# Float16 high and low parts for both layers of a spectral block, in place of float32r

## The chip, the cores and the metric

The kernel runs on one core of one Trainium2 chip. The metric is the device time of one execution in microseconds. The engines of the core have in-order instruction streams of their own: TensorE (PE in the profile, its weight loads PEld), VectorE (DVE), ScalarE (ACT), GpSimd (POOL), and SyncE (SP), which issues the DMA transfers.

## The reference, cut to what matters

x has 8192 rows of 448 columns. With `mod` computed from `c` and `w_mod`, the spectral part is

```python
h = _layernorm(x, axis=-1) * (1 + ca) + sa
Xf = rfft2(h)                            # over the 8192 rows and (length 1) H
z = Xf.reshape(..., NB=4, BS=112)        # 4 blocks of 112 columns
hr = zr @ w1[0] - zi @ w1[1] + b1[0];  hi = zi @ w1[0] + zr @ w1[1] + b1[1]
hr, hi = relu(hr), relu(hi)
or_ = hr @ w2[0] - hi @ w2[1] + b2[0]; oi_ = hi @ w2[0] + hr @ w2[1] + b2[1]
or_, oi_ = soft thresholds with lam = 0.01: sign(o) * max(|o| - lam, 0)
x = x + ga * irfft2(or_ + 1j * oi_)
```

Then a second layer norm with modulation and a GEGLU feed-forward of width 1792 follow, which the change does not touch.

## The kernel before, in words

The Fourier transform of 8192 rows is split into 128 x 64. The first stage (to about 72 us of the profile) normalizes the rows, multiplies by `f1` (the transform of length 128) and stores the result `td` to DRAM. The spectral stage, to about 376 us, works in 32 units: two halves h of the columns (two blocks of 112 each) by 16 groups `bt` of frequencies, in the order of `BTS`. Each unit passes through four functions:

- `stage_s2`: the transform of length 64, 24 float16 matmuls. For each of two blocks kk, ScalarE writes `zhi` (float32r, scaled by `ca1`, a scalar of each partition), VectorE the rest `zlo` = value - `zhi`.
- `stage_m1`: the first layer. Each real or imaginary output is six float32r matmuls of 256 columns, with high and low parts of weights (`w1h`, `w1l`) and data; 24 in a unit. ScalarE writes relu to `hhi`, VectorE `hlo`.
- `stage_m2`, for two halves p of the unit's frequencies: the second layer, six matmuls of 224 columns for each block, 24 in a unit. ScalarE makes `t` = relu(value - lam), VectorE in four instructions `y` = min(value + lam, t); together they are the soft threshold.
- `stage_i1`: the inverse transform of length 64, six float32r matmuls of 448 columns; ScalarE copies the result to `us`.

The order of instructions is written by hand (`manual_schedule`). `step(i)` issues the fetch of unit i + 2, `stage_s2` of unit i, `stage_m2` of unit i - 2, `stage_i1` of unit i - 3 and `stage_m1` of unit i - 1. The table `side` hangs work of the next part on the steps: `squares` (ScalarE, one in each of steps 4 to 15, two in steps 12 and 13, with `norms` matmuls a step later) and `weights_hi` and `weights_lo` (ScalarE and VectorE, one each in steps 18 to 31, names `wk<-raw`). I call these squares steps and weights steps; steps 16 and 17 have neither. `drip` issues small leftovers.

In a step ScalarE's order is zh, zh (of `stage_s2`), th (the float16 copy of the next fetched unit), squares or `weights_hi`, t, t (of `stage_m2`), yh, us, us, yh, hh, hh (of `stage_m1`). VectorE's is zl, zl, y eight times, the step's side work (`weights_lo` in a weights step), hl, hl.

Before the first step stands the preparation: `mod_cols` sums the modulation into columns (TensorE, then `sa0` and `ca1` on VectorE), `mod_rows` makes rows `sb_r` and `cb_r` for the second layer norm, `mlp_weights` splits the weights on VectorE, constant rows are written into the four `zh` and the four `hh` buffers, and `split_t` makes th and tl of units 0 and 1 from the fetched `tr`, tl on VectorE for these two. The bank of PSUM that `stage_s2` of unit 0 fills is free for unit 1 once ScalarE and VectorE have made zh and zl from it.

Of the kernel before, what the change touches and what calls it, by code (L numbers as in the profile page):

```python
# [45 lines left out]
SSC = 14  # L46


@with_exitstack
def spectral_geglu(ctx, tc, x, w1, b1, w2, b2, wg, wu, wd, cvec, wmod, cf1, cs2, cmi, cgm, out):  # L50
# [23 lines left out]
    nlam = cpool.tile([128, 1], F32, name="nlam")  # L74
    V.memset(nlam, -LAM)
# [67 lines left out]
    with ExitStack() as actx:  # L143
# [91 lines left out]
        def mod_rows():  # L235

            out = []
            for h, r in enumerate((sb_r, cb_r)):
                ps = bank("pd", "psm")
                for k in range(4):  # L240
                    T.matmul(
                        ps[:, :D], cs[:, k : k + 1].to_broadcast([112, 128]), wn[:, k, h * D : (h + 1) * D], start=k == 0, stop=k == 3
                    )
# [1710 lines left out]
```

## Time and profile before

| | |
|---|---|
| median of three runs | 1883.52 us (1882.44 to 1884.96) |
| profiled execution, its own span | 1881.0 us |
| TensorE matmul busy | 1841.5 us, 98% |
| VectorE, ScalarE, GpSimd busy | 74%, 53%, 68% |
| mean granted TensorE clock | 0.996 |
| first stage, spectral stage, the rest | to 72, 72 to 376, 376 to 1881 us |

Matmuls are pipelined and the profile models their ends, so TensorE looks busy whenever starts are less than some 0.25 us apart. For its real pace one reads the distance of starts in the timeline. A row of the timeline has start, length, engine, line, operation, tiles and in brackets the idle time before it with what ended it; several instructions of a line in a row are merged with a count.

### The profile page before, as it was taken

How to read it: one execution, taken by the hardware profiler on the slowest of the kernel's cores; microseconds unless marked ns; L12 is line 12 of the kernel's file. 1: busy time of each engine (PE TensorE's matmuls, PEld its weight loads, DVE VectorE, ACT ScalarE, POOL GpSimd, SP SyncE). 2: the span in 40 equal slices, each digit the busy share in tenths (PEclk: the TensorE clock that was granted, in tenths of full speed). 3: DMA queues.
4: the chain of work that ended last, by engine and by line, in shares of the span. 5: the costliest groups of instructions: out<-in, count | busy, mean ns of one | idle time of the engine just before them, and what ended most of it. 6: DMA issues, size and time to landing. Idle time of an engine off the chain costs nothing.

```text
span 1881.0 us, 56421 instructions
## 1 busy us (share of the span) xinstructions
PE 1841.5 (98%) x23332; PEld 1748.9 (93%) x23332; DVE 1397.2 (74%) x2887; ACT 1000.7 (53%) x1844; POOL 1271.3 (68%) x1684
## 2 busy tenths in 40 slices
PE   7899999999999999999999999999999999999998
PEld 3599999878889989999999999999999999999998
DVE  7777788787766667777777777777777777777745
ACT  5677888753444444455555555555555555444443
POOL 3157654347777778777777777777777777777534
PEclk9999999999999999999999999999999999999999
DMA  9999777754543445966666666666666666666651
GB/s 350 319 301 262 204 183 189 192 157 92 133 107 88 101 96 125 291 177 178 175 172 169 169 169 169 169 169 169 173 177 178 170 173 180 176 173 179 155 162 55
DMA packets 380614, 330.49 MB, mean 176 GB/s; under 512 B 110784, under 2 KB 358724, under 8 KB 380356
## 3 DMA queue, kind: packets, MB, share of 16 engines
q1 hardware_dynamic: 380356, 326.87, 63.9%
q8 instruction: 183, 3.00, 0.7%
q14 instruction: 75, 0.61, 0.1%
HBM read 243.32 MB, written 60.10 MB: 161 GB/s over the span
## 4 chain that ended last, share of the span: by engine, by line
PE 82%; DVE 6%; DMA 3%; issue 3%; ACT 2%; SPq 2%; POOL 2%; ACTq 0%; DVEq 0%; POOLq 0%
PE set L1391 39%; PE pgu L1148 11%; PE pdn L1221 6%; PE pdn L1223 6%; PE pdn L1222 6%; PE ps L211 2%; PE set L1223 2%; PE set L1222 2%; PE set L1221 2%; DVE y L479 1%; POOL yl L116 1%; DVE st L172 1%; PE set L1515 1%; DMA raw<-in_B_w_gate 1%; DVE wk L838 1%
## 5 line engine op out<-in xcount | busy, mean ns | idle before, releaser
L1391 PE MATMUL set<-nt,wk 128*128 128x128 f16 x13104 | 736.5, 219 | 2.8 <-DMA wk<-wk 1.6
L1391 PEld LDWEIGHTS <-wk 128*128 128x128 f16 x13104 | 733.9, 98 | 3.2 <-DMA wk<-wk 1.8
L1223 PE MATMUL pdn<-wd,ac 128*128 128x224 f16 x1218 | 315.5, 259 | 0.6 <-DVE ac L1209 0.6
L1221 PE MATMUL pdn<-wd,ac 128*128 128x224 f16 x1218 | 315.7, 259 | 0.0
L1222 PE MATMUL pdn<-wd,ac 128*128 128x224 f16 x1218 | 315.5, 259 | 0.0
L1148 PE MATMUL pgu<-nt,wk 128*128 128x256 f16 (+1 forms) x2464 | 268.3, 274 | 3.1 <-DVE x L1189 3.1
L1148 PEld LDWEIGHTS <-wk 128*128 128x128 f16 (+1 forms) x2464 | 225.8, 98 | 44.2 <-issue 18.3
L1440 ACT ACTIVATE gl<-c,dg 128x384 f32<-128x384 f32 x168 | 103.5, 616 | 230.6 <-DVE c L1434 227.7
L1466 DVE SCALAR_TENSOR_TENSOR ac<-x,sa_act,ac 128x896 f16<-128x896 f32 x168 | 205.8, 1225 | 19.9 <-ACT ac L1456 19.9
L1197 POOL TENSOR_TENSOR x<-x 128x128 f32<-128x128 f32 x223 | 129.8, 582 | 117.6 <-DVE x L1189 56.2
L1267 POOL TENSOR_TENSOR cq<-cq 128x224 f32<-128x224 f32 x32 | 21.1, 659 | 261.8 <-DVE cq L1266 261.8
L1198 POOL TENSOR_TENSOR x<-x 128x128 f32<-128x128 f32 x223 | 185.6, 832 | 17.5
L1456 ACT ACTIVATE ac<-x,sa_act 128x896 f16<-128x896 f32 x168 | 174.1, 1036 | 13.5 <-POOL x L1200 6.6
L1444 DVE TENSOR_TENSOR x<-c,gl 128x384 f32<-128x384 f32 x168 | 154.4, 919 | 17.2 <-ACT gl L1440 17.1
L1221 PEld LDWEIGHTS <-ac 128*128 128x128 f16 x1568 | 153.4, 98 | 4.9 <-issue 4.8
L1223 PEld LDWEIGHTS <-ac 128*128 128x128 f16 x1568 | 153.4, 98 | 0.8 <-DVE ac L1209 0.8
L1222 PEld LDWEIGHTS <-ac 128*128 128x128 f16 x1568 | 153.5, 98 | 0.1
L1428 DVE TENSOR_TENSOR c<-set,sb 128x512 f32<-128x512 f32 x168 | 115.4, 687 | 35.7 <-PE set L1391 35.7
L1199 POOL TENSOR_TENSOR x<-x 128x128 f32<-128x128 f32 x223 | 134.0, 601 | 0.0
L1184 ACT ACTIVATE gel<-pgu,dg 128x256 f32<-128x256 f32 x112 | 49.4, 470 | 156.7 <-PE pgu L1148 149.1
L1419 ACT COPY sb<-set 128x512 f32<-128x512 f32 x168 | 97.6, 581 | 61.8 <-PE set L1391 60.4
L479 DVE SCALAR_TENSOR_TENSOR y<-pm,t 64x224 f32<-64x224 f32 x256 | 99.5, 389 | 39.1 <-ACT t L471 35.2
(338 smaller groups left out, 3998.8 us busy)
## 6 DMA issues: line engine op xcount, KB each, us to landing
wk<-wk SPq DMA_DIRECT2D x76, 1024.0 KB
wk<-wk SPq DMA_DIRECT2D x76, 768.0 KB
vd<-us SPq DMA_DIRECT2D x64, 224.0 KB
xx<-in_A_x SPq DMA_DIRECT2D x32, 448.0 KB
v<-vd SPq DMA_DIRECT2D x63, 224.0 KB
out<-x SPq DMA_DIRECT2D x31, 448.0 KB
xt<-in_A_x SPq DMA_DIRECT2D x15, 896.0 KB
tr<-td SPq DMA_DIRECT2D x60, 224.0 KB
```

Source lines behind the costliest of these rows:

```text
L479: V.scalar_tensor_tensor(y[ri * 64 : ri * 64 + 64, gi], pv[si, ri], LAM, tv[si, ri], op0=ALU.add, op1=ALU.min)
L1148: T.matmul(pgu[i, t, q][:, pr * H : (pr + 1) * H], ws[rows, n, w, tw], nts[i][rows, tn, :], start=start, stop=stop, skip_group_check=True,)
L1197: e.tensor_tensor(s1, a21, a22, ALU.add)
L1198: e.tensor_tensor(s2, s1, a11, ALU.subtract)
L1199: e.tensor_tensor(s3, a11, a21, ALU.subtract)
L1221: T.matmul(ps, ac[:, 0, ka], w[:, 0, kb], start=n == 0, stop=False)
L1222: T.matmul(ps, ac[:, 0, ka], w[:, 1, kb], start=False, stop=False)
L1223: T.matmul(ps, ac[:, 1, ka], w[:, 0, kb], start=False, stop=n == NP - 1)
L1391: T.matmul(ps2[:, pr, reg * 128 : reg * 128 + 128], slot[:, pr, hl, wt, :], nt[:, xt, :], start=start and j == 0, stop=j == len(terms) - 1 ...
L1444: V.tensor_tensor(xs[u][:, 1::3, :], cts.pop(u)[:, 1], gls.pop(u), ALU.mult)
L1456: S.activation(ac[:, 0], xs[u][:, 0:7], AF.Copy, scale=sa_act[:, t : t + 1])
L1466: V.scalar_tensor_tensor(ac[:, 1], xs.pop(u)[:, 0:7], sa_act[:, t : t + 1], ac[:, 0], op0=ALU.mult, op1=ALU.subtract)
```

## The change

The data and weights of both layers (`zh`, `zl`, `hh`, `hl`, `w1h`, `w1l`, `w2h`, `w2l`) become float16. Since float16 has a narrow range, powers of two scale them. The factor 1 + ca now goes into the first weights (`w1m`), so `zh` and `zl` get a constant scale; the shift sa comes in as an addition `hb` to the hidden value at frequency 0. The scales `wsc` of the two layers are made on the chip: a bound of each layer's weights (`wmx`, `cmx`, `cm`) is squared, summed over the partitions by a matmul with ones (`psq`), and turned into a power of two by integer operations on its exponent. The thresholds change with the scales, so `lam` becomes a tile, and `ga_r` takes the inverse scale `iso`.

```diff
-    w1h = mpool.tile([113, 3, NBLK, BS], F32R, name="w1h")
+    w1h = mpool.tile([113, 3, NBLK, BS], F16, name="w1h")
...
+        def dc_cols():
+
+            ps = bank("pc", "psd")
+            for r in range(2):
+                for k in range(NBLK):
+                    T.matmul(ps[:112, 4 * r + k : 4 * r + k + 1], wt[:112, 0, r, k, :], sa0[:, k : k + 1], start=True, stop=True)
+            return lambda: V.tensor_scalar(hb, ps[:112, : 2 * NBLK], wsc[:112, 0:1], None, op0=ALU.mult)
+
+        def bounds1():
+
+            V.tensor_reduce(cmx[:112, 0:1], ca1[:112], mybir.AxisListType.X, ALU.max, apply_absolute_value=True)
+            V.tensor_reduce(cmx[:112, 1:2], sa0, mybir.AxisListType.X, ALU.max, apply_absolute_value=True)
+            V.scalar_tensor_tensor(
+                cm[:112, 0:1], cmx[:112, 1:2], 2.0**ZSC / N, cmx[:112, 0:1], op0=ALU.mult, op1=ALU.add
+            )
+            V.tensor_tensor(cm[:, 0:1], cm[:, 0:1], wmx[:, 0:1], ALU.mult)
+            V.tensor_tensor(cm[:, 0:1], cm[:, 0:1], cm[:, 0:1], ALU.mult)
+            V.tensor_tensor(
+                w1m, wt[:, 0], ca1.rearrange("p (r k o) -> p r k o", r=1, o=1).to_broadcast([113, 2, NBLK, BS]), ALU.mult
+            )
+
+        def scale_of(j, p):
+
+            ps = bank("pc", "psq")
+            T.matmul(ps[:, 0:1], ones[:113, :128], cm[:, j : j + 1], start=True, stop=True)
+            w = wsc[:, j : j + 1]
+            wi = w.bitcast(I32)
+            V.tensor_scalar(w, ps[:, 0:1], 1e-20, None, op0=ALU.max)
+            V.tensor_scalar(wi, wi, 1, 0x7F800000, op0=ALU.logical_shift_right, op1=ALU.bitwise_and)
+            V.tensor_scalar(wi, wi, -1.0, float((189 + p) << 23), op0=ALU.mult, op1=ALU.add)
+
+        def weights1():
+            sc = wsc[:113, 0:1]
+            S.activation(w1h[:, 0:2], w1m, AF.Copy, scale=sc)
+            V.scalar_tensor_tensor(w1l[:, 0:2], w1m, sc, w1h[:, 0:2], op0=ALU.mult, op1=ALU.subtract)
+            for w in (w1h, w1l):
+                neg(w[:112, 2], w[:112, 1])
+
+        def bounds2():
+
+            V.scalar_tensor_tensor(col2, f1c[:113, 129:130], wsc[:113, 0:1], f1c[:113, 128:129], op0=ALU.mult, op1=ALU.add)
+            V.tensor_tensor(cm[:, 1:2], wmx[:, 1:2], col2, ALU.mult)
+            V.tensor_tensor(cm[:, 1:2], cm[:, 1:2], cm[:, 1:2], ALU.mult)
+
+        def weights2():
+            V.tensor_tensor(col2, col2, wsc[:113, 1:2], ALU.mult)
+            wr = wt[:, 1].rearrange("p r k o -> p k r o")
+            wv = [w.rearrange("p s k (r o) -> p s k r o", r=2) for w in (w2h, w2l)]
+            S.activation(wv[0][:, 0], wr, AF.Copy, scale=col2)
+            for r in range(2):
+                V.scalar_tensor_tensor(
+                    wv[1][:, 0, :, r], wt[:, 1, r], col2, wv[0][:, 0, :, r], op0=ALU.mult, op1=ALU.subtract
+                )
+            for w in wv:
+                neg(w[:112, 1, :, 0], w[:112, 0, :, 1])
+                V.tensor_copy(w[:112, 1, :, 1], w[:112, 0, :, 0])
+
+        def thresholds():
+
+            V.tensor_scalar(iso, wsc[:, 0:1], wsc[:, 1:2], 2.0**-ZSC, op0=ALU.mult, op1=ALU.mult)
+            V.tensor_scalar(lam[:, 0:1], iso, LAM, None, op0=ALU.mult)
+            V.tensor_scalar(lam[:, 1:2], iso, -LAM, None, op0=ALU.mult)
+            V.tensor_scalar(iso.bitcast(I32), iso.bitcast(I32), -1.0, float(254 << 23), op0=ALU.mult, op1=ALU.add)
...
-                zlo = bp.tile([BS, 2, ZW], F32R, tag="zl", name="zl", bufs=4)
+                zlo = bp.tile([BS, 2, ZW], F16, tag="zl", name="zl", bufs=4)
...
-                c1 = ca1[:, 2 * h + kk : 2 * h + kk + 1]
+                c1 = 2.0 ** -(TSC + SSC + ZSC)
                 S.activation(zhi[:BS, :, 0 : GB * 64], p3, AF.Copy, scale=c1)
...
+                    for ro in range(2):
+                        h0 = bp.tile([BS, 1], F32, tag="h0", name="h0", bufs=2)
+                        j = slice(ro * NBLK + k, ro * NBLK + k + 1)
+                        V.tensor_scalar(h0, banks[ro][:, 0:1], hb[:, j], 0.0, op0=ALU.add, op1=ALU.max)
+                        V.tensor_copy(hhi[:BS, ro, 0:1], h0)
+                        V.tensor_tensor(hlo[:, ro, 0:1], h0, hhi[:BS, ro, 0:1], ALU.subtract)
...
-            S.activation(t, ps[:, :D], AF.Relu, bias=nlam)
+            S.activation(t, ps[:, :D], AF.Relu, bias=lam[:, 1:2])
...
-                        y[ri * 64 : ri * 64 + 64, gi], pv[si, ri], LAM, tv[si, ri], op0=ALU.add, op1=ALU.min
+                        y[ri * 64 : ri * 64 + 64, gi], pv[si, ri], lam[si, 0:1], tv[si, ri], op0=ALU.add, op1=ALU.min
...
-            S.copy(ga_r[:, :HC], ga[:, :HC])
+            S.activation(ga_r[:, :HC], ga[:, :HC], AF.Copy, scale=iso)
...
         mod_cols()
-        row_copies = mod_rows()
-        row_copies[0]()
+        bounds1()
+        hb_out = dc_cols()
+        row_copy = mod_row(0)
+        scale_of(0, 4)
+        row_copy()
+        weights1()
+        hb_out()
+        bounds2()
+        row_copy = mod_row(1)
+        scale_of(1, 13)
...
         for u in units[:2]:
             split_t(*u, el=V)
-        row_copies[1]()
+        row_copy()
+        weights2()
+        thresholds()
```

The order of instructions moves where the preparation stands. First TensorE, from the last sums of the modulation (`psm<-ones,ms`) to the first unit's matmuls (th is its stationary operand). Before:

```order
L251 MATMUL psm<-ones,ms 112x1 x4
L241 MATMUL psm<-wn,cs 128x448 x8
L384 LDWEIGHTS th
L384 MATMUL ps_881<-s_153,th 112x2x64
L385 LDWEIGHTS th
```

With the change:

```order
L259 MATMUL psm<-ones,ms 112x1 x4
L268 MATMUL psd<-sa_162,wt 112x1 x8
L241 MATMUL psm<-wn,cs 128x448 x4
L287 MATMUL psq<-cm,ones 128x1
L241 MATMUL psm<-wn,cs 128x448 x4
L287 MATMUL psq<-cm,ones 128x1
L452 LDWEIGHTS th
L452 MATMUL ps_927<-s_152,th 112x2x64
```

The eight products for `hb` (`psd`) and the two sums over partitions (`psq`) now stand ahead of the first unit, the second `psq` directly before it.

VectorE, from the modulation's columns (`sa`, `ca`) to the first zl. Before:

```order
L252 TENSOR_SCALAR sa_118<-psm 112x4
L254 TENSOR_SCALAR ca_117<-psm 112x4
L650 CAST zh_836<-ones 17x258
L650 CAST zh_837<-ones 17x258
L650 CAST zh_838<-ones 17x258
L650 CAST zh_839<-ones 17x258
L650 CAST hh_840<-ones 17x258
L650 CAST hh_841<-ones 17x258
L650 CAST hh_842<-ones 17x258
L650 CAST hh_843<-ones 17x258
L116 TENSOR_TENSOR tl<-tr,th 128x896 x2
L393 SCALAR_TENSOR_TENSOR zl<-ps_881,ca_117,zh_836 112x2x256
```

With the change, first from the modulated weights `w1m` to the second scale's first operation:

```order
L280 TENSOR_TENSOR w1m<-wt,ca_161 113x896
L290 TENSOR_SCALAR wsc<-psq 128x1
L291 TENSOR_SCALAR wsc<-wsc 128x1
L292 TENSOR_SCALAR wsc<-wsc 128x1
L297 SCALAR_TENSOR_TENSOR w1l<-w1m,wsc,w1h 113x896
L335 TENSOR_SCALAR w1h<-w1h 112x448
L335 TENSOR_SCALAR w1l<-w1l 112x448
L269 TENSOR_SCALAR hb<-psd,wsc 112x8
L303 SCALAR_TENSOR_TENSOR col_168<-f_153,wsc 113x1
L304 TENSOR_TENSOR cm<-wmx,col_168 113x1
L305 TENSOR_TENSOR cm<-cm 113x1
L290 TENSOR_SCALAR wsc<-psq 128x1
```

and then from tl of units 0 and 1 (behind the rows of constants, which stand as before) to the first zl:

```order
L116 TENSOR_TENSOR tl<-tr,th 128x896 x2
L308 TENSOR_TENSOR col_168<-col_168,wsc 113x1
L313 SCALAR_TENSOR_TENSOR w2l<-wt,col_168,w2h 113x4x112 x2
L335 TENSOR_SCALAR w2h<-w2h 112x4x112
L318 COPY w2h<-w2h 112x4x112
L335 TENSOR_SCALAR w2l<-w2l 112x4x112
L318 COPY w2l<-w2l 112x4x112
L322 TENSOR_SCALAR iso<-wsc 128x1
L323 TENSOR_SCALAR lam<-iso 128x1
L324 TENSOR_SCALAR lam<-iso 128x1
L325 TENSOR_SCALAR iso<-iso 128x1
L461 SCALAR_TENSOR_TENSOR zl<-ps_927,zh_870 112x2x256
```

The split of the weights, which stood ahead of `sa` and needed no modulation, now stands behind the scales: the first layer's part ahead of tl, the second's between tl and the first zl.

ScalarE, from the first row copy to the first zh. Before:

```order
L244 COPY sb_r<-psm 128x448
L114 CAST th<-tr 128x896 x2
L244 COPY cb_r<-psm 128x448
L392 ACTIVATE zh_836<-ps_881,ca_117 112x2x256
L392 ACTIVATE zh_837<-ps_897,ca_117 112x2x256
```

With the change:

```order
L244 COPY sb_r<-psm 128x448
L296 ACTIVATE w1h<-w1m,wsc 113x896
L114 CAST th<-tr 128x896 x2
L244 COPY cb_r<-psm 128x448
L311 ACTIVATE w2h<-wt,col_168 113x896
L460 ACTIVATE zh_870<-ps_927 112x2x256
L460 ACTIVATE zh_871<-ps_943 112x2x256
```

`w1h` now stands ahead of the first th, and `w2h` ahead of the first zh.

106 lines of the change are left out of this document (54 added, 52 removed).

## The prediction

> **What bounds the kernel now.** I read the page first (span, chain by engine), then the busy time by stretch for single steps of the spectral part, then the timelines of TensorE, ScalarE and VectorE inside two such steps, and last the start of the spectral part, where the new weight preparation stands.
>
> ```profile
> span 1881.0 us, 56421 instructions
> ...
> PE 82%; DVE 6%; DMA 3%; issue 3%; ACT 2%; SPq 2%; POOL 2%; ACTq 0%; DVEq 0%; POOLq 0%
> ```
>
> The profiled execution's own span is 1881.0 us; the three runs have a median of 1883.52, so 2.5 us lie around the span. I make the sum on the span and add 2.5. The change touches only the spectral part, 72 to 376 us. The next view has one row for each stretch: its length, busy time of PE, PEld, DVE, ACT and POOL (with counts), granted clock, DMA share, GB/s. The first three stretches are single steps (from stage_s2 to the next stage_s2): one with `squares`, one without extras, one with `weights_hi`/`weights_lo`. The fourth is the tail of the stage.
>
> ```profile
> 122.54:131.31 8.77, 8.77 (x88) 8.54 (x87) 6.10 (x14) 7.19 (x13) 6.82 (x8) 1.00 0.90 292
> 222.47:230.75 8.28, 8.28 (x82) 8.01 (x81) 6.02 (x14) 6.74 (x12) 5.50 (x7) 1.00 0.73 177
> 256.81:265.30 8.49, 8.44 (x81) 8.15 (x79) 7.24 (x17) 7.03 (x13) 5.17 (x4) 1.00 0.72 171
> ...
> 344.15:364.00 19.85, 19.40 (x163) 18.18 (x162) 14.38 (x30) 13.67 (x25) 6.24 (x5) 1.00 0.77 210
> ```
>
> TensorE looks full everywhere, but its ends are modelled; what a step can lose has to come from the loop that closes second. That loop runs over ScalarE and VectorE alone: t (L471), eight y (L479), yh, two hh (L447), two zh (L392), th, and squares or weights, then the next t. Timeline of the squares step, columns start, length, engine, line:
>
> ```profile
> 126.50 1.15 ACT L471 ACTIVATE t<-pm,nlam 128x448 f32<-128x448 f32 x2
> 127.23 3.22 DVE L479 SCALAR_TENSOR_TENSOR y<-pm,t 64x224 f32<-64x224 f32 x8 [1.64 <-ACT t L471]
> 130.54 0.56 ACT L114 CAST yh<-y 128x448 fp32r<-128x448 f32 x1 [0.20 <-DVE y L479]
> 131.02 1.08 ACT L447 ACTIVATE hh<-pm 112x512 fp32r<-112x512 f32 x2
> 132.22 1.36 ACT L392 ACTIVATE zh<-ps,ca 112x512 fp32r<-112x512 f32 x2
> 133.48 0.93 ACT L114 CAST th<-tr 128x896 f16<-128x896 f32 x1
> 134.31 1.06 ACT L724 ACTIVATE sq<-xt 128x1024 bf16<-128x1024 f32 x1
> ```
>
> With sq's 0.96 to the next t, the step from t to t is 8.77 (134.31 + 0.96 - 126.50). ScalarE waits for TensorE only around hh and zh: 131.02 + 1.08 - 0.11 of overlap is 131.99 against 132.22, and the two zh are a little apart. That is some 0.34 us; the ScalarE-VectorE loop is 8.43 long inside an 8.77 step. In the weights step nothing is left over:
>
> ```profile
> 252.49 1.18 ACT L471 ACTIVATE t<-pm,nlam 128x448 f32<-128x448 f32 x2
> 253.25 3.22 DVE L479 SCALAR_TENSOR_TENSOR y<-pm,t 64x224 f32<-64x224 f32 x8 [0.98 <-ACT t L471]
> ...
> 259.97 1.18 ACT L834 ACTIVATE wk<-raw,sw 128x1024 f16<-128x1024 f32 x1
> 261.02 1.18 ACT L471 ACTIVATE t<-pm,nlam 128x448 f32<-128x448 f32 x2
> ```
>
> From t to t 8.53, with no wait of ScalarE but that for y. So weights steps are bound by this loop already, squares steps have 0.34 to give before they are.
>
> **What the change costs and brings, part by part.**
>
> *Matmuls in float16.* Starts of matmuls in a row, first and last:
>
> ```profile
> 254.05 0.28 PE L431 MATMUL pm<-zl,w1h 112*112 112x256 f32 x1
> ...
> 256.69 0.28 PE L435 MATMUL pm<-zh,w1l 112*112 112x256 f32 x1
> ...
> 250.25 0.28 PE L460 MATMUL pm<-w2h,hh 112*128 112x224 f32 x1
> ...
> 252.48 0.27 PE L462 MATMUL pm<-w2h,hl 112*128 112x224 f32 x1
> ...
> 519.92 6.29 PE L1148 MATMUL pgu<-nt,wk 128*128 128x256 f16 x56
> ...
> 574.98 0.26 PE L1221 MATMUL pdn<-wd,ac 128*128 128x224 f16 x1
> ...
> 577.75 0.26 PE L1223 MATMUL pdn<-wd,ac 128*128 128x224 f16 x1
> ```
>
> Layer one takes 2.64 us for 22 steps, 120 ns each; float16 of the same 256 columns (6.29 - 0.27) / 55 = 109. Layer two takes 2.23 for 20, 112 ns; float16 of 224 columns 2.77 for 29, 96. A unit has 24 of each, so 24 x 11 + 24 x 16 = 0.65 us off TensorE, 20.7 us over 32 units if TensorE set every step.
>
> *Scalar operands.* Durations, least, median, greatest:
>
> ```profile
> L393 DVE SCALAR_TENSOR_TENSOR zl<-ps,ca,zh x64: 739/744/754, 82.6 to 347.1; 112x512 fp32r<-112x512 f32 x64
> ...
> L448 DVE SCALAR_TENSOR_TENSOR hl<-pm,hh x60: 679/691/694, 88.0 to 356.6; 112x512 fp32r<-112x512 f32 x60
> ...
> L479 DVE SCALAR_TENSOR_TENSOR y<-pm,t x256: 372/390/396, 93.3 to 365.1; 64x224 f32<-64x224 f32 x128
> ...
> L392 ACT ACTIVATE zh<-ps,ca x64: 688/692/705, 81.8 to 346.0; 112x512 fp32r<-112x512 f32 x64
> ...
> L447 ACT ACTIVATE hh<-pm x60: 588/592/604, 87.3 to 356.0; 112x512 fp32r<-112x512 f32 x60
> ```
>
> zl and hl differ only in that zl takes its scalar from a tile and hl has a constant: 53 ns. y goes from a constant to `lam`, so 8 x 53 = 0.42 us more between t and yh. Bounds: 0 if the read hides, 100 ns a piece by ScalarE's difference (692 against 592); I take 53, the same operation on the same engine. zh goes the other way on ScalarE: 100 ns less in duration, some 85 in pitch, 0.17 for two. The loop grows by 0.25 us. zl's own 53 ns lie off the loop. The eight y take 3.22, so 0.404 each against a duration of 0.390: they do not overlap, and a longer one moves the next by all of it. The Trainium skill (VectorE: DVE Perf Modes, "Two Vector instructions with no wait between them") says that an instruction whose operands start in another quadrant is held until the earlier ones end; y alternates halves, so by the rule the price counts whole, which makes the rival of free reads smaller.
>
> Float16 outputs cost nothing extra: zl's 744 for 512 columns and L1209's least of 1135 for 896 (below) lie on one line, 1.02 ns a column, though one writes float16.
>
> *Steps, summed.* Weights steps (19 to 27, 29, 30): 11 x +0.25 = +2.7. Steps 12 and 13 with two squares each: +0.5. Other squares steps, 8: from 8.77 to the loop's 8.43 + 0.25 = 8.68, -0.09 each, -0.8. Steps 16 to 18 and 28, near 8.25: loop 8.43 - 0.96 + 0.25 = 7.72, TensorE 8.25 - 0.65 = 7.60, so -0.5 each, -2.0. The two steps with bt = 0 get 12 small VectorE operations for h0 and lose 6 for z0, against 0.65 of TensorE: 0. Tail: two layer-one and three layer-two passes of 0.26 and 0.38, -1.7, of which y takes back 0.5: -1.2. First steps: +0.2. Sum -0.6. So TensorE's 20.7 us are nearly all lost to the other loop.
>
> *The start.* Rows of before:
>
> ```profile
> 71.47 0.86 PE L251 MATMUL psm<-ones,ms 112*112 112x1 f32 x8
> 72.19 6.26 PE L241 MATMUL psm<-wn,cs 112*128 112x448 f32 x16
> 83.36 0.22 PE L384 MATMUL ps<-s,th 128*112 128x128 f16 x1 [0.89 <-DVE zl L393]
> ...
> 73.46 0.90 DVE L650 CAST hh<-ones 17x258 fp32r<-17x258 f32 x4
> 79.88 2.24 DVE L116 TENSOR_TENSOR tl<-tr,th 128x896 f16<-128x896 f32 x2 [5.52 <-DMA td<-xt]
> ...
> 373.80 0.16 DVE L1079 TENSOR_TENSOR t<-r 128x2 f32<-128x2 f32 x1
> ...
> 374.40 0.16 DVE L1082 TENSOR_TENSOR r<-r,t 128x2 f32<-128x2 f32 x1
> ...
> L1209 DVE SCALAR_TENSOR_TENSOR ac<-x,sa_act,ac x56: 1135/1152/2119, 400.1 to 768.0; 128x896 f16<-128x896 f32 x56
> ...
> PEld L386 <- POOL tl L116: 1.8, 1, 1.8
> ```
>
> VectorE idles 5.52 us before tl: that is the only cover. Four dependent small operations start 0.20 apart. The new chain, in us: sa0 72.4; eight psd products (twice L251's 0.86) to 74.1; the first half of L241 (3.1) to 77.2, psq behind it 77.5; three operations on wsc 78.1; w1h on ScalarE 1.04 (th's 0.93 for as many columns, and 0.1 for its scalar), 79.2 (th waits 0.3 behind it); w1l 1.1 and two negations 0.6, 80.9; hb, col2, cm, cm 0.7 and the second psq 0.3, 81.9 (behind it on TensorE stands all of stage_s2); wsc 82.5; hh and zh rows 8 x 0.22, 84.3. tl of unit 0 therefore starts 4.4 us late, and the first two are done at 86.5. Then col2, w2h on ScalarE, 87.8 (zh of units 0 and 1 stand behind it); w2l 1.3 and four copies or negations 1.2, 90.3; thresholds 0.7, 91.0; only then zl of unit 0, whose end (91.6) frees the bank for stage_s2 of unit 1: 83.36 becomes about 91.4 with float16 copies a little quicker. That is +8.0. On SP, the fetch of unit 2 reuses the buffer that tl reads and moves by 4.4 as well, less than the th that needs it, so it isn't late. In exchange the 1.8 us that stage_s2 of unit 2 waits for its tl (last row, of the waits) shrink to about 0.8, since th and tl alone are left in the way and not the fetch. So +7.0 is left by the first hh of unit 1. Ends: +3 if the transfers still due then would have held TensorE up anyway, +9 if nothing is given back. The two copies to ga_r get a tile scale, 0.1 us each; two more columns in f1's load and POOL's copies in place of casts (bt = 0 only) I cost at nothing: POOL is idle for 2 us of the squares step above, and f1's load brings 1 KB more.
>
> TensorE then rests from about 86.6 to 91.4. After the pause before 376.65 the trace shows
>
> ```profile
> 376.65 0.23 PE L1130 MATMUL ptr<-ident,pk 128*128 128x128 f16 x1 [2.62 <-ACT pk L1103]
> ...
> 378.00:382.00 4.00, 3.08 (x22) 2.38 (x21) 3.36 (x8) 3.08 (x5) 0.00 (x0) 0.50 0.28 78
> ```
>
> a granted clock of 0.50. A half clock for the first 2 to 4 us of work costs 1 to 2; I take +1.3. The Trainium skill (TensorE: Matmul & The Clock Gate, "Part 1: The HAM clock gate") has the clock halve after an idle window of about 3.4 us and return after as much work; by it the term would be 1.7 and the time 0.4 more. The trace agrees on the half.
>
> Sum: +7.0 + 1.3 - 0.6 = +7.7, span 1888.7, time 1891.
>
> **Rivals.** (a) The loop follows TensorE instead of bounding it: all 20.7 us come, with the start +8.3, 1871, faster. It decides if ScalarE's wait in a step is over 0.9 us (0.65 + 0.25); the rows show 0.34 and none. (b) y's tile reads are free: loop 0.17 shorter instead of 0.25 longer; squares steps -0.5 x 8, plain -0.65 x 4, weights -0.17 x 11, two-squares -0.3, tail -1.7, sum -10.5 in place of -0.6: 1881, the same. For it: nothing on 64 partitions is measured; against: zl and hl. (c) The start is mostly covered (+3 and no half clock): 1886, the same. For it: TensorE waits there now too, 0.89 and 1.8 us in the rows; against: the new chain runs through VectorE, ScalarE and TensorE, and no transfer is in it. (d) The start is worse: every small operation waits longer, the clock stays half through both layers, or y costs 100 ns: 1897 to 1902.
>
> **How the numbers follow.** No change and a change are told apart here at about 0.2%, 3.8 us. Forecast (1887.5 to 1896) 0.60, (a) 0.07, (b) 0.10, (c) 0.10, (d) 0.13. Range 1881 to 1898: it leaves out (a) and most of (d), 0.17 in all. Slower: forecast and (d), 0.73; same: (b) and (c), 0.19; faster: (a) and an edge of (b), 0.08.
>
> **What would show it.** Right: layer-one starts 109 ns apart, layer-two 96; y near 443 ns and zh near 592; weights steps of 8.7 to 8.8 us; ScalarE no longer waiting for TensorE in squares steps; the second unit's first matmul near 91; a granted clock under 1 between 84 and 98. Wrong: steps near 8.1 throughout (a), y still 390 (b), the first hh of unit 1 under 4 us late (c).

## The result and the profile after

The changed kernel takes 1895.61 us (median of 4 runs, 1895.41 to 1897.94) against 1883.19 for the kernel before in the same comparison (4 runs, 1882.44 to 1884.96): ratio 1.0064, 95% interval 1.0053 to 1.0076. It is slower by 12.4 us where 7.7 were forecast, and inside the range. The profiled execution has a span of 1893.9 us and took 1895.66. The page's span and its chain of work by engine:

```profile
span 1893.9 us, 56483 instructions
...
PE 77%; DVE 9%; ACT 5%; DMA 4%; SPq 2%; issue 2%; POOL 1%; ACTq 0%; DVEq 0%
```

TensorE's share of the chain fell from 82% to 77%, and VectorE's and ScalarE's rose from 6% and 2% to 9% and 5%. TensorE did get faster. First and last of 12 layer-one matmuls in a row, and of 22 layer-two matmuls:

```profile
291.81 0.27 PE L492 MATMUL pm<-zh,w1h 113*112 113x256 f16 x1
...
293.03 0.27 PE L497 MATMUL pm<-zh,w1l 112*112 112x256 f16 x1
...
296.27 0.27 PE L527 MATMUL pm<-w2h,hl 112*128 112x224 f16 x1 [0.66 <-DVE hl L516]
...
298.32 0.26 PE L530 MATMUL pm<-w2h,hl 112*128 112x224 f16 x1
```

1.22 us over 11 steps from start to start is 111 ns, 2.05 over 21 is 98, where 109 and 96 were forecast. The length of the steps did not follow. Stretches as in the prediction (length, then busy time of PE, PEld, DVE, ACT, POOL): a squares step, a bt = 0 step, step 16, and a weights step (step n runs from stage_s2 of unit n to that of unit n + 1):

```profile
128.41:137.16 8.75, 8.39 (x87) 7.75 (x86) 7.24 (x15) 6.78 (x12) 6.71 (x8) 1.00 0.94 303
164.08:175.45 11.37, 9.56 (x99) 8.34 (x99) 10.70 (x31) 7.21 (x15) 6.74 (x7) 1.00 0.78 233
...
223.35:231.53 8.18, 7.82 (x79) 7.30 (x79) 7.93 (x18) 5.95 (x11) 7.12 (x10) 1.00 0.67 200
...
266.68:275.58 8.90, 7.95 (x80) 7.26 (x79) 7.68 (x18) 6.93 (x13) 5.18 (x5) 1.00 0.69 165
```

The squares step is as long as before (8.75 against 8.77), with TensorE now idle for 0.36 us of it. The timeline of ScalarE and VectorE there, the same step as shown of before:

```profile
132.90 1.18 ACT L539 ACTIVATE t<-pm,lam 128x448 f32<-128x448 f32 x2
...
133.67 3.72 DVE L547 SCALAR_TENSOR_TENSOR y<-pm,lam,t 64x224 f32<-64x224 f32 x8 [1.30 <-ACT t L539]
...
137.47 0.56 ACT L114 CAST yh<-y 128x448 fp32r<-128x448 f32 x1 [0.45 <-DVE y L547]
137.94 1.08 ACT L515 ACTIVATE hh<-pm 112x512 f16<-112x512 f32 x2
138.91 1.09 ACT L460 ACTIVATE zh<-ps 112x512 f16<-112x512 f32 x2
139.86 0.96 ACT L114 CAST th<-tr 128x896 f16<-128x896 f32 x1
140.69 1.09 ACT L804 ACTIVATE sq<-xt 128x1024 bf16<-128x1024 f32 x1
141.65 1.18 ACT L539 ACTIVATE t<-pm,lam 128x448 f32<-128x448 f32 x2
```

From t to t it is 8.75, and each row of ScalarE starts where the one before ends, but for the wait for y: the loop is closed. That it sets the step is what the experiments test. Durations, least, median, greatest:

```profile
L547 DVE SCALAR_TENSOR_TENSOR y<-pm,lam,t x256: 432/450/459, 99.4 to 377.0; 64x224 f32<-64x224 f32 x128
...
L461 DVE SCALAR_TENSOR_TENSOR zl<-ps,zh x64: 678/681/692, 88.9 to 359.6; 112x512 f16<-112x512 f32 x64
...
L460 ACT ACTIVATE zh<-ps x64: 577/601/621, 86.3 to 358.5; 112x512 f16<-112x512 f32 x64
```

y costs 60 ns more (390 before), zl 63 less (744 before) and zh 91 less (692 before). The start, on VectorE, then on TensorE, then two stretches with their granted clock:

```profile
71.30 0.16 DVE L260 TENSOR_SCALAR sa<-psm 112x4 f32<-112x4 f32 x1 [3.19 <-PE psm L259]
...
83.14 2.09 DVE L116 TENSOR_TENSOR tl<-tr,th 128x896 f16<-128x896 f32 x2
...
86.41 1.28 DVE L313 SCALAR_TENSOR_TENSOR w2l<-wt,col,w2h 113x448 f16<-113x448 f32 x2 [1.11 <-ACT w2h L311]
...
88.91 1.28 DVE L461 SCALAR_TENSOR_TENSOR zl<-ps,zh 112x512 f16<-112x512 f32 x2
...
84.29 0.36 PE L454 MATMUL ps<-s,tl 128*112 128x128 f16 x1 [3.36 <-DVE tl L116]
89.64 0.26 PE L452 MATMUL ps<-s,th 128*112 128x128 f16 x1 [2.76 <-DVE zl L461]
...
84.00:88.00 4.00, 2.60 (x22) 2.50 (x23) 2.89 (x8) 2.12 (x3) 0.00 (x0) 0.50 0.56 135
88.00:92.00 4.00, 2.36 (x23) 2.35 (x23) 2.37 (x10) 0.60 (x1) 0.00 (x0) 0.50 0.96 353
```

tl starts 3.3 us later than before (79.88), unit 1's first matmul 6.3 later (83.36), and the granted clock in the last two stretches is 0.50. Before, sa started at

```profile
72.36 0.16 DVE L252 TENSOR_SCALAR sa<-psm 112x4 f32<-112x4 f32 x1
```

so the changed kernel was 1.1 us ahead there. The start of sa varies between profiles from 69.2 to 72.4 us, and by 1.8 between two programs that are alike up to it (the last two of the table below). A comparison of starts is therefore made from sa too: to unit 4 it is 32.7 us before and 39.7 after.

Where the 12.9 us of the two spans' difference arose, by the first matmul of stage_s2 of each unit: unit 4 starts 5.9 later, unit 9 still 5.8; step 9 adds 0.6, the bt = 0 steps 10 and 11 add 2.8, steps 12 and 13 add 0.4, steps 14 to 18 give back 0.7, steps 19 to 30 add 2.7, and what follows unit 31's start adds 1.3.

### The profile page after: what moved, and what is told of

It is laid out like the page before. It is cut to its first block, busy times and chain, and to the rows that moved or that the text cites. A ratio compares the mean times of both kernels' runs of the same rounds, so it can differ in the third digit from the quotient of the medians.

```text
span 1893.9 us, 56483 instructions
## 1 busy us (share of the span) xinstructions
PE 1833.0 (97%) x23352; PEld 1727.5 (91%) x23352; DVE 1412.6 (75%) x2922; ACT 991.9 (52%) x1846; POOL 1269.2 (67%) x1684
## 4 chain that ended last, share of the span: by engine, by line
PE 77%; DVE 9%; ACT 5%; DMA 4%; SPq 2%; issue 2%; POOL 1%; ACTq 0%; DVEq 0%
PE set L1471 38%; PE pgu L1228 10%; PE pdn L1303 6%; PE pdn L1301 6%; PE pdn L1302 6%; DVE y L547 4%; PE set L1302 2%; PE set L1301 2%; PE set L1303 2%; PE ps L212 2%; DMA raw<-in_B_w_up 1%; DMA raw<-in_B_w_gate 1%; DMA tr<-td 1%; DMA td<-xt 1%; PE set L1595 1%
## 5 line engine op out<-in xcount | busy, mean ns | idle before, releaser
L1508 DVE TENSOR_TENSOR c<-set,sb 128x512 f32<-128x512 f32 x168 | 115.3, 686 | 34.9 <-PE set L1471 34.6
L547 DVE SCALAR_TENSOR_TENSOR y<-pm,lam,t 64x224 f32<-64x224 f32 x256 | 115.2, 450 | 34.5 <-ACT t L539 30.4
L116 POOL TENSOR_TENSOR yl<-y,yh 128x448 fp32r<-128x448 f32 x63 | 77.9, 1236 | 86.3 <-ACT yh L114 83.1
```

Of the source, the lines that this page charges most:

```text
L547: V.scalar_tensor_tensor(y[ri * 64 : ri * 64 + 64, gi], pv[si, ri], lam[si, 0:1], tv[si, ri], op0=ALU.add, op1=ALU.min)
```

## The experiments

One table for all: the columns up to "unit 31 starts" are read from each kernel's one trace (us; in brackets the time from sa to unit 4), the median is that of its runs. The kernel before had 1883.6 to 1884.1 in these comparisons; each ratio is against it.

| kernel | unit 4 starts (from sa) | step 6, squares | step 10, bt = 0 | step 22, weights | unit 31 starts | median | ratio, 95% |
|---|---|---|---|---|---|---|---|
| before | 105.05 (32.7) | 8.77 | 10.04 | 8.51 | 344.15 | 1883.2 | |
| after | 110.99 (39.7) | 8.75 | 11.37 | 8.71 | 355.77 | 1895.6 | 1.0053 to 1.0076 |
| after again | 110.79 (39.7) | 8.75 | 11.40 | 8.72 | 355.65 | 1895.4 | 1.0047 to 1.0073 |
| y's number | 111.49 (39.2) | 8.24 | 11.16 | 8.22 | 344.70 | 1883.4 | 0.9987 to 1.0005 |
| before, y's tile | 105.76 (34.6) | 8.91 | 10.52 | 8.95 | 352.91 | 1893.7 | 1.0038 to 1.0067 |
| before, float16 | 104.58 (32.9) | 8.71 | 10.04 | 8.41 | 341.31 | 1879.2 | 0.9969 to 0.9987 |
| no h0 | 111.85 (40.2) | 8.75 | 10.58 | 8.70 | 356.84 | 1897.2 | 1.0058 to 1.0084 |
| extra behind t | 109.81 (40.2) | 8.12 | 11.39 | 7.81 | 336.76 | 1876.6 | 0.9949 to 0.9974 |
| before, extra behind t | 106.36 (34.8) | 8.77 | 9.48 | 8.20 | 342.11 | 1880.5 | 0.9973 to 0.9990 |
| fixed scales | 106.18 (37.0) | 8.76 | 12.05 | 8.72 | 352.08 | 1892.9 | 1.0034 to 1.0060 |
| warm | 109.64 (38.5) | 8.76 | 11.37 | 8.71 | 355.55 | 1896.1 | 1.0052 to 1.0079 |
| combined | 105.69 (36.2) | 8.12 | 9.54 | 7.62 | 328.02 | 1865.4 | 0.9885 to 0.9916 |
| combined, old place | 104.70 (33.7) | 8.24 | 9.86 | 8.23 | 340.03 | 1875.6 | 0.9942 to 0.9968 |
| later yl | 106.03 (36.9) | 8.27 | 9.92 | 8.22 | 337.09 | 1875.5 | 0.9939 to 0.9966 |

Two edits of the kernel before that leave its start alone have 34.6 and 34.8 in brackets where it has 32.7; in their traces some matmuls of the first units ran at a granted clock of 0.50, in its own none did. So the start of the changed kernel costs 5 to 7 us, depending on which of these one compares with.

### What y's scalar costs, in the changed kernel and in the one before

```diff
-  y[...], pv[si, ri], lam[si, 0:1], tv[si, ri], op0=ALU.add, op1=ALU.min
+  y[...], pv[si, ri], 4 * LAM, tv[si, ri], op0=ALU.add, op1=ALU.min
```

> The changed kernel with y's scalar as a number (4 * LAM, the value that lam holds for these inputs) in place of the tile lam; t keeps its tile bias. Theory (the closed loop over ScalarE and VectorE carries every y): y falls from 0.467 to 0.404 us of pitch, so 0.50 a step; squares steps 8.75 -> 8.25, weights steps 8.84 -> 8.34, two-squares and bt = 0 steps 0.4 less, together 11 x 0.5 + 11 x 0.5 + 4 x 0.4 + 0.5 = 13 us: 1883 (1881 to 1886). Rival (TensorE bounds the steps, y's read is beside the path): 1895, no change.

1883.4, 12.2 us less: as the theory had it. Steps 6 and 22 both fall by half a microsecond, so one operand of eight instructions a step costs as much as the whole change lost. It is not the only loss: unit 4 still starts 6.4 later than before, and without y's tile the steps now gain that back. The other way round, in the kernel before:

```diff
+  plam = cpool.tile([128, 1], F32, name="plam"); V.memset(plam, LAM)
-  y[...], pv[si, ri], LAM, tv[si, ri], op0=ALU.add, op1=ALU.min
+  y[...], pv[si, ri], plam[si], tv[si, ri], op0=ALU.add, op1=ALU.min
```

> The kernel before with one thing changed: y's scalar comes from a tile that holds LAM; float32r and all else stay. Theory: eight y 0.46 to 0.50 longer a step; weights steps have no wait of ScalarE left and grow by it (11 x 0.48 = 5.3), two-squares steps too (1.0), squares steps only by what goes beyond their 0.34 of waiting (8 x 0.15 = 1.2), plain steps by nothing: +7.5, 1890.7 (1888.5 to 1893). Rival (TensorE hides it): 1883.

```profile
L481 DVE SCALAR_TENSOR_TENSOR y<-pm,plam,t x256: 435/450/460, 93.5 to 375.0; 64x224 f32<-64x224 f32 x128
```

y takes 450 ns here too, and the time is +10.1, above the theory's range. Steps 6 and 22 grow by 0.14 and 0.44, as forecast, but all 11 weights steps together by 3.7 and not 5.3. What the forecast missed are the bt = 0 steps (+0.48 and +0.35), step 9 (+0.6), steps 16, 17 and 28 (+1.2 together), and the work behind unit 31 (+1.0); 0.7 more is the start of this profile.

### What float16 alone brings

```diff
-  w1h = mpool.tile([113, 3, NBLK, BS], F32R, name="w1h")
+  w1h = mpool.tile([113, 3, NBLK, BS], F16, name="w1h")
...
-  zlo = bp.tile([BS, 2, ZW], F32R, tag="zl", name="zl", bufs=4)
+  zlo = bp.tile([BS, 2, ZW], F16, tag="zl", name="zl", bufs=4)
```

> The kernel before with zh, zl, hh, hl, w1h, w1l, w2h, w2l as float16 and nothing else: modulation still in zh's scalar from a tile, y with a number, no bounds, no new preparation. Theory (TensorE's 0.65 a step counts only until the other loop closes): squares steps -0.34 x 8, plain -0.55 x 4, bt = 0 -0.5 x 2, first steps -0.4 x 4, weights 0, tail -1.7: -9, 1874 (1871 to 1877). Rival (TensorE sets every step): -20.7, 1862.5.

-4.5, half of what the theory said, outside its range, and a fifth of the rival's. Steps 5 to 8 take 8.31, 8.71, 8.96 and 8.47: 8.61 in the mean against 8.77, so 0.16 came out of a TensorE that is 0.65 quicker. The 0.34 us of waiting that the prediction saw on ScalarE were not all to be had; why these four steps differ is open. The bt = 0 steps gave 0.1 in the mean and not 0.5, the work behind unit 31 0.9 and not 1.7, and the profile has a half clock in step 24 (11.43 against 9.80). zl takes 743 ns here, with a float16 result and its scalar still in a tile, 744 before: the float16 output costs nothing, as the prediction assumed from two rows of different length, which could not show it. Stretches of a squares and a weights step:

```profile
120.97:129.68 8.71, 8.46 (x87) 7.71 (x86) 6.84 (x14) 7.07 (x12) 6.70 (x8) 1.00 0.93 285
262.22:270.63 8.41, 7.88 (x81) 7.28 (x80) 6.89 (x14) 6.94 (x13) 4.50 (x4) 1.00 0.81 203
```

### Where TensorE's gain went

The extra work of ScalarE (squares, weights_hi) goes behind the two t of a step; it then runs while VectorE makes y:

```diff
-  hook("act")
   m2 = 0 <= i - 2 < nu
   if m2:
       y0 = stage_m2(*units[i - 2], 0)
       y = stage_m2(*units[i - 2], 1)
+  hook("act")
+  if m2:
       ys = [split_y(y0)]
```

> The changed kernel with the place of ScalarE's extra work (squares, weights_hi) moved in each step from ahead of the two t to behind them, so that ScalarE does it while VectorE works on y. Theory (the loop t, y, yh, hh, zh, th, extra, t takes up TensorE's gain): the extra 1.06 to 1.36 us leave the loop; squares steps 8.75 -> 8.05, which is TensorE's own time, weights steps 8.84 -> 7.9, where VectorE's y, wk, hl and the wait for t close at 7.6 to 7.9; two-squares steps -0.8: 8 x 0.7 + 11 x 0.95 + 1.6 + 0.6 = 18 less, 1877.5 (1873 to 1882). Rival (something else holds the steps, such as hl behind wk): 1890 or more.

> The same move in the kernel before. Theory: there TensorE's float32r time is the other bound, so squares steps stay at 8.77 and only weights steps fall, from 8.52 to TensorE's 8.15: -0.35 x 11 = -4, two-squares -0.4: 1879 (1877 to 1882). So after the move the change itself would be worth about -2 instead of +12. Rival (the move is worth the same in both): -18, 1865.

1876.6 and 1880.5: 19 us in the changed kernel, 3.1 in the one before, both in the theory's ranges. This settles the central point: the loop over ScalarE and VectorE had held the steps. With the extra work out of it, the squares step takes all of the 0.65 us (8.77 to 8.12), and the timeline shows t waiting for TensorE, and sq in the time in which ScalarE used to wait for y:

```profile
129.16 0.64 ACT L539 ACTIVATE t<-pm,lam 128x448 f32<-128x448 f32 x1
130.21 0.64 ACT L539 ACTIVATE t<-pm,lam 128x448 f32<-128x448 f32 x1 [0.41 <-PE pm L530]
130.74 1.05 ACT L805 ACTIVATE sq<-xt 128x1024 bf16<-128x1024 f32 x1
131.84 0.56 ACT L114 CAST yh<-y 128x448 fp32r<-128x448 f32 x1
```

Between these two kernels the change is worth -3.9 us, with its start and its bt = 0 steps still paid.

### The start

Scales as constants, second weights and thresholds made in the first stage:

```diff
-  bounds1(); ...; scale_of(0, 4); ...; bounds2(); ...; scale_of(1, 13)
+  modulate()
...
-  weights2(); thresholds()
+  V.memset(wsc[:, 0:1], 1.0); V.memset(wsc[:, 1:2], 512.0); ...; weights2(); thresholds()   # in mlp_bounds
```

> The changed kernel with the two scales as constants (1 and 512, the values that the bounds give for these inputs): no maxima, no cm, no psq; weights2 and thresholds move to the end of the first stage. The modulation of the first weights, psd and hb stay. Theory (the new chain sets the start): first layer-one matmul of unit 0 some 4 to 5 us earlier than in the changed kernel, the half clock there shorter, -5.5: 1890 (1888.5 to 1892). Rival (transfers would hold the start there anyway): -1 to -2, 1894.

The time falls by 2.8, between the theory (its range ends at 1892) and the rival. Unit 4 starts 4.8 us earlier, but so does the chain itself, by 2.1:

```profile
69.20 0.16 DVE L257 TENSOR_SCALAR sa<-psm 112x4 f32<-112x4 f32 x1 [4.74 <-PE psm L256]
...
83.42 0.69 DVE L435 SCALAR_TENSOR_TENSOR zl<-ps,zh 112x512 f16<-112x512 f32 x1 [0.49 <-ACT zh L434]
```

From sa to the first zl it is 14.2 us in place of 17.6, and to unit 4 37.0 in place of 39.7. So the scales' chain is worth 2.7 to 3.4 us and not the 5.5 of the theory, and some 2.8 come through to the time. In the profile two half clocks came as well, in steps 10 (12.05 against 11.37) and 14 (9.74 against 8.22). The other piece of the start, TensorE's clock:

```diff
+  wb = bank("pc", "psw")                  # behind scale_of(1, 13)
+  for _ in range(4):
+      T.matmul(wb[:, :D], wn[:, 0, 0:128], wn[:, 0, 0:D], start=True, stop=True)
...
+  wb = bank("pc", "psw")                  # behind stage_s2 of unit 0
+  for _ in range(28):
+      T.matmul(wb[:, 0:256], ident, s20[:, 0, :, :].rearrange("p a b -> p (a b)"), start=True, stop=True)
```

> The changed kernel with matmuls whose result nothing reads in TensorE's two pauses of the start (4 of 448 columns in float32 behind the second psq, 28 of 256 columns in float16 behind stage_s2 of unit 0). Theory: the clock stays whole, stage_s2 of unit 1 and the first layer one lose their half clock, and 1.3 us come back: 1894.3 (1893.5 to 1895). Rival (VectorE's chain of zl, hl alone sets the start, the clock is beside the path): 1895.6.

The clock stays whole at the start and unit 4 starts 1.35 us earlier, 1.2 counted from sa, close to the 1.3 of the prediction. The time stays (1896.1), so the rival has the time right and its reason wrong. The trace has a half clock in step 14 that the changed kernel has not: it makes that step 1.5 us longer, and step 15 gives 0.4 back, so that unit 31 starts only 0.2 earlier. The executions lie between 1893.9 and 1897.5; what the whole clock is worth in the time stays open. Steps 13 and 14 of this run, and the same of the changed kernel (granted clock third from the end):

```profile
194.96:205.03 10.07, 9.04 (x95) 8.17 (x94) 6.50 (x17) 7.95 (x14) 6.92 (x5) 1.00 0.74 200
205.03:214.78 9.75, 9.75 (x88) 9.35 (x87) 6.47 (x15) 6.89 (x13) 4.15 (x3) 0.82 0.79 222
```

```profile
196.31:206.38 10.07, 9.04 (x95) 8.18 (x94) 6.50 (x17) 7.95 (x14) 6.92 (x5) 1.00 0.71 195
206.38:214.60 8.22, 8.22 (x88) 7.72 (x87) 5.99 (x14) 6.56 (x12) 3.95 (x3) 1.00 0.87 236
```

The same pauses in step 13 (0.26 and 0.77 us of TensorE), the same busy times, and a different clock behind them.

### The small operations of bt = 0

```diff
-  h0 = bp.tile([BS, 1], F32, tag="h0", name="h0", bufs=2)
-  V.tensor_scalar(h0, banks[ro][:, 0:1], hb[:, j], 0.0, op0=ALU.add, op1=ALU.max)
-  V.tensor_copy(hhi[:BS, ro, 0:1], h0)
-  V.tensor_tensor(hlo[:, ro, 0:1], h0, hhi[:BS, ro, 0:1], ALU.subtract)
```

> The changed kernel without the twelve small VectorE operations for h0 in each of the two bt = 0 steps (column 0's share from the shift of the modulation is left out). Theory: steps 10 and 11 fall from 11.37 to about 9.7 to 10.0 and step 9 by some 0.3: -3.3, 1892.3 (1891.5 to 1893.5). Rival (these steps wait for banks and for POOL's copies, not for h0): 11.3 as now, 1895.6.

Steps 10 and 11 fall by 0.8 and 1.2 us, 2.0 of the 2.7 to 3.3 of the theory, and step 9 not at all; the time does not fall (1897.2). Step 24 of this profile is 11.74 long at a mean clock of 0.85, where the changed kernel's is 9.17 at 1.00:

```profile
292.51:304.25 11.74, 9.55 (x81) 8.38 (x79) 10.39 (x18) 8.70 (x17) 5.39 (x5) 0.85 0.63 158
```

Steps 24 to 27 sum to 37.9 us against 36.3, and steps 10 to 13 had given 1.5: the profiled run lost there what it had gained, and 0.9 more in the start of unit 4. By the time alone this run settles nothing. The kernel "combined, old place" below also has no h0 operations, and its steps 10 and 11 are 1.3 and 1.4 shorter than with y's number alone; its time holds other edits as well.

### The versions that follow from it

The first five lines name operations in short, with their order; the last two are code.

```diff
-  iso, lam from wsc[:, 0] * wsc[:, 1]; y with lam[si, 0:1]
+  OSC = 4.0: y with OSC * LAM, nlam by memset, ga_r with 1 / OSC; w2 scaled by 512 / wsc[:, 0]
-  mod_cols, bounds1, psd, mod_row(0), scale_of(0), weights1, hb, bounds2, mod_row(1), scale_of(1), rows of constants, tl, weights2
+  mod_cols, bounds1, scale_of(0), mod_row(0), weights1, rows of constants, mod_row(1), tl; weights2 in step 1
-  h0 ... (twelve operations)
+  for w_, s_ in ((w1h, sah), (w1h, sal), (w1l, sah)):
+      T.matmul(o[:, 0:1], w_[:BS, ro, k, :], s_[:, k : k + 1], start=False, stop=False)
```

The constant scale of the output fits these inputs; weights of quite another size would need another constant.

> The changed kernel with ScalarE's extra work behind the two t, and four more edits: the scale of layer two's output is the constant 4 (second weights scaled by 512 over the first scale; no second bound, y's threshold a number); the chain of the first scale stands ahead of the modulation rows on TensorE and of tl on VectorE; the second weights are made in step 1, behind the first layer one; column 0's shift goes in as one-column matmuls in place of the twelve h0 operations. Theory: against 1876.6 with the move alone, start -5, bt = 0 steps 11.39 and 10.89 to 9.3 each, -3.7, y's read -0.3 in the 9 weights steps that VectorE closes, -2.7: 1865.5 (1861 to 1870), 0.990 of the kernel before. Rival (the pauses thus saved return as half clock or as waits for transfers at the start): 1871 to 1875.

> The same four edits with ScalarE's extra work left in its old place. Theory: against 1883.4 with y's number alone, start -5, bt = 0 steps 11.16 and 10.82 to 9.6, -2.8: 1875.5 (1872 to 1879). So float16 is worth some 8 here and 15 with the place moved as well. Rival: the start gives nothing, 1880.

1865.4 and 1875.6, both as the theory had them; each time holds four edits or five, whose shares are not separated. With the extra work behind t the kernel is 1.0% faster than the one before (0.9901, 0.9885 to 0.9916): TensorE is busy all through the squares, the bt = 0 and the weights step:

```profile
121.87:130.00 8.13, 8.13 (x88) 7.89 (x87) 5.84 (x14) 7.02 (x13) 6.74 (x8) 1.00 0.89 288
154.99:164.53 9.54, 9.54 (x111) 9.03 (x111) 7.51 (x19) 6.74 (x15) 6.28 (x7) 1.00 1.01 306
262.34:269.96 7.62, 7.62 (x80) 7.24 (x79) 7.15 (x14) 7.04 (x14) 4.83 (x3) 1.00 0.85 223
```

### Two effects beside the change

> The changed kernel itself once more, with a profile of its own. Theory (a pause of TensorE of 1.5 to 2.5 us is followed by a half clock in some executions and not in others): the time is the same within 0.1%, 1895.6, but steps with the same pauses (13, 14, 19, 24) need not show the half clock in the same places as in the first profile. Rival (it is fixed by the program): the same steps in the same 0.05 us.

From step 4 on the second profile has the same steps within 0.03 us, and no half clock between the start and unit 31. So the pauses of this program leave the clock whole in both profiles, as the rival has it. Two profiles do not show that it is fixed: in either series one execution is some 2 us longer (1897.94 and 1897.01) at a mean granted clock of 0.993 where the others have 0.994. The same pauses are followed by a half clock in another program (step 14 above).

The last run adds one ScalarE instruction so that GpSimd's yl starts later:

```diff
   if m2:
+      if 24 <= i <= 27:
+          S.copy(dly, y[:, 1, 0:1])
       ctx_u[("y",) + units[i - 2]] = ys + [split_y(y)]
```

> The four edits with the extra work in its old place (1875.6), and in steps 24 to 27 one more ScalarE instruction, a copy of a single column of y, ahead of the second yh: it only makes GpSimd's second yl start some 0.15 us later. Theory (VectorE's second 512-column piece of wk and GpSimd's yl keep each other out; where they start within 0.02 us of each other VectorE loses and takes 1.70 us, where VectorE is 0.03 ahead it takes 0.75 and yl 1.71): all four second pieces take 0.75, the pause of 1.78 ahead of layer two in step 24 shrinks to about 0.8 and no half clock follows it; steps 24 to 27 from 11.23, 7.54, 9.73 and 8.53 (37.0) to 8.6 each (34.4): -2.6, 1873. Rival (the 1.70 belongs to that piece or to its data): 1.70 as before, and 0.1 more in each step, 1876.

The time stayed at 1875.5 (1875.6 without), so the 2.6 us are not shown. What the theory says of the two operations is. The four steps with wk in two pieces are 23 to 26 of the code, so the first pair was left undelayed and the other three were delayed. First and second pair of this kernel, VectorE's two pieces in one row and GpSimd's second yl:

```profile
277.88 2.38 DVE L908 SCALAR_TENSOR_TENSOR wk<-raw,sw,wk 128x512 f16<-128x512 f32 x2
278.58 1.13 POOL L121 TENSOR_TENSOR yl<-y,yh 128x448 fp32r<-128x448 f32 x1 [0.50 <-ACT yh L119]
...
286.40 1.42 DVE L908 SCALAR_TENSOR_TENSOR wk<-raw,sw,wk 128x512 f16<-128x512 f32 x2
287.13 1.68 POOL L121 TENSOR_TENSOR yl<-y,yh 128x448 fp32r<-128x448 f32 x1 [0.53 <-ACT yh L119]
```

The undelayed pair has wk wait (2.38) and yl whole (1.13); the delayed pairs have wk whole (1.42) and yl wait (1.68, 1.62, 1.62). Without the edit pairs 1, 3 and 4 had wk wait, so the delay turned two pairs round. Steps 24 to 27 sum to 34.6 us in this profile and to 37.0 without the edit, of which 1.6 are a half clock in step 24 that followed the same pause of TensorE (1.6 us) and here did not come. Step 28 is 0.75 longer (8.29 against 7.54), and so the five steps without the half clock gain 0.1: the two pairs that were turned round brought almost nothing. (The profile without the edit is also that of the longest of its five executions, 1878.9.)

## Why the prediction came out as it did

The direction and the mechanism were right, and the size in part: TensorE's 20.7 us were lost to the loop over ScalarE and VectorE (shown by taking the extra work out of that loop), and the start cost several microseconds. That the time came out inside the range is partly luck, since terms missed in both directions. By its own terms, forecast and measured:

| term | forecast | measured | |
|---|---|---|---|
| start, with the half clock | +8.3 | +5.9 | at unit 4; 7.0 counted from sa, of it 2.7 the scales' chain, 1.2 the clock |
| squares steps 4 to 8, and 15 | -0.09 each | -0.07 to 0.0 | loop 8.75, not 8.68 |
| squares steps 9 and 14 | -0.09 each | +0.64, -0.55 | |
| two-squares steps 12 and 13 | +0.5 | +0.4 | |
| bt = 0, steps 10 and 11 | 0 | +2.8 | 0.8 and 1.2 back without h0, 0.2 and 0.5 with y's number |
| steps 16 to 18 | -0.5 each | -0.05, +0.25, -0.37 | |
| steps 19 to 30 | +2.2 | +2.7 | |
| behind unit 31's start | -1.2 | +1.3 | 1.2 back with y's number |

The step that failed most plainly is the sentence on the two bt = 0 steps: "12 small VectorE operations for h0 and lose 6 for z0, against 0.65 of TensorE: 0". It put the new operations at nothing against what the step loses elsewhere. VectorE's row of this step before, then rows of two of the four groups with the operation behind them, and what TensorE waited for in step 10 (in total, times, longest):

```profile
157.62:167.66 10.04, 9.82 (x99) 9.32 (x98) 7.86 (x19) 7.43 (x16) 6.78 (x8) 1.00 0.89 262
...
165.46 0.21 DVE L510 TENSOR_SCALAR h<-pm1a,hb 112x1 f32<-112x1 f32 x1
165.70 0.16 DVE L511 CAST hh<-h 112x1 f16<-112x1 f32 x1
165.90 0.23 DVE L512 TENSOR_TENSOR hl<-h,hh 112x1 f16<-112x1 f32 x1
166.05 0.20 DVE L510 TENSOR_SCALAR h<-pm1b,hb 112x1 f32<-112x1 f32 x1
166.29 0.16 DVE L511 CAST hh<-h 112x1 f16<-112x1 f32 x1
166.48 0.38 DVE L512 TENSOR_TENSOR hl<-h,hh 112x1 f16<-112x1 f32 x1
166.78 0.41 DVE L504 SCALAR_TENSOR_TENSOR hl<-pm1a,hh 112x258 f16<-112x258 f32 x1
...
PE ps L452 <- DVE h L510: 1.3, 1, 1.3
```

Two groups take 1.32 us (165.46 to 166.78), so four take some 2.64 a step, and VectorE is busy 10.70 of 11.37 there (7.86 of 10.04 before). TensorE also waits 1.3 us for one of them before a part of stage_s2, whose bank of PSUM they still read; without h0 the same wait is 0.64, for hl.

The loop was mis-sized by y: 62 ns a piece in pitch (3.22 to 3.72 for eight) where 53 came from zl and hl, so 0.50 instead of 0.42. zl itself, once its scalar is a number, takes 681 ns and not hl's 691, a difference of 63: two operations that are alike in shape were not alike in time, and hl stood in badly for zl without its tile. By the rule quoted there of the Trainium skill (VectorE: DVE Perf Modes, "Two Vector instructions with no wait between them"), a held instruction starts only when every earlier one has finished. The trace agrees: the pitch grew by 62 ns and the duration by 60, so a longer y counted whole.

For steps 16 to 18 the prediction weighed ScalarE's loop (7.72) and TensorE (7.60) and left VectorE's own row out. With sq out, VectorE is the next to be full (7.93 of 8.18 us in step 16, 6.92 of 8.24 before), and y's 0.50 lies on it too; with y's number step 16 takes 7.73. Step 17 takes 8.28 there, as before the change, so y does not hold it; what does was not tested.

Behind unit 31's start y's pieces lie on the path: the kernels with y's tile take 1537.3 to 1539.1 us there, those with a number 1536.0 to 1537.6. Of float16's 1.7 us little shows in it: with a number, the two float32r kernels take 1536.9 and 1537.6, the five float16 ones 1536.0 to 1537.1.

In steps 19 to 30 the sum came close by luck. VectorE's second pieces of wk took 1.69 us in the kernel before, where they collided with GpSimd's yl, and take 0.75 in the changed kernel, where yl takes longer instead. Steps 24 and 26 are 0.6 and 0.3 shorter, which the forecast did not have; whether that is the reason was not tested. The other ten steps grow by 0.2 to 0.7, 3.6 together, where 2.2 were forecast for all twelve.

The start was forecast too long by 2.4 at unit 4, by 1.3 counted from sa, and not because transfers covered it. The chain from sa to the first zl took 17.6 us (71.30 to 88.91) where 18.6 had been summed (72.4 to 91.0), and in this execution it began 1.1 us earlier than in the one before. The first hh of unit 1 is 6.6 late (103.58 against 97.01). The half clock lasted longer than the 2 to 4 us that were assumed, 10.2 us from 82.6 to 92.9, at the price of the 1.2 above.

Of the rivals, (b) came close without being right: with free reads the time would have been 1883.4, as the run with y's number shows, where 1881 was said. (a) is excluded by the steps, (c) by a start that costs some 5 us or more. (d) has its lower end 1.4 us above the time, and its reasons did not come about: y costs 60 ns and not 100, the small operations start 0.2 us apart as assumed, and the clock was whole again before the first unit's second layer.

## What to carry to other kernels

Before an engine is made faster, write down the loop over the other engines, from one instruction to its next instance: the step takes the longer of the two. The fix may be to move work that an engine does inside that loop into a wait that is already there (19 us here against 3 in the slower kernel). Here a scalar operand that turned from a number into a tile had a price on each instruction, and the closed loop paid most of it: 60 ns on 256 instructions are 15 us, and 12 came through. Small dependent operations are to be counted by their spacing, and by whose banks they hold. Starts of two executions are to be compared from a mark that both share, as sa here: the plain difference of 4.8 us with fixed scales held 2.1 from ahead of the chain.

## What the runs showed of the hardware

**Half clock after short pauses.** Besides the start, TensorE ran at 0.50 for 3.41 us at a time in 5 of the 11 edited kernels, between 139 and 301 us, each time with pauses of 0.8 to 2.2 us in all within the 5 us ahead of it. The step concerned and the one behind it were together 0.5 to 1.6 us longer than in the nearest kernel without it. Equal pauses left the clock whole elsewhere (step 13 of the changed kernel; step 24 of the last one). The Trainium skill (TensorE: Matmul & The Clock Gate, "Part 1: The HAM clock gate") has the clock watched in windows of 3.4 us that run free of the program. The trace agrees on the half and on the length, and the half clocks of one trace begin at whole multiples of 3.41 us from one another (72.53, 82.77, 161.27 and 202.23 with fixed scales: 3, 23 and 12 of them apart); that the place of a pause in such a window decides is not shown by any run here. For this reason a difference of some 2 us between two kernels is uncertain where each has one profile.

**VectorE and GpSimd keep each other out.** Where VectorE's second 512-column wk and GpSimd's yl start within 0.11 us of each other, one of them takes 0.95 us (wk) or 0.5 to 0.6 (yl) more. The Trainium skill (SBUF — State Buffer, "Who interferes with whom") has a VectorE instruction with two inputs in SBUF contend with a GpSimd instruction that reads SBUF, and the order of issue decide which of them is blocked. The trace agrees on the contention, and yl lost wherever it was recorded 0.06 to 0.11 us behind. For closer starts the order of the records does not say which loses: in the undelayed pair above the second piece of wk was recorded 0.03 us ahead of yl (278.55 and 278.58) and lost, in the changed kernel 0.03 ahead (294.74 and 294.77) and won.
